# Spreading one small row over the partitions: a repeating DMA in place of a product with ones, a copy and a fill

## The chip, the cores and the metric

The kernel runs on one core of one Trainium2 chip. The profile names the core's parts: PE (matrix products; PEld is its weight load), DVE, ACT and POOL (elementwise engines), SP (it only issues transfers here), and 16 DMA engines that move data between HBM and the on-chip memories. ACT, POOL and SP each issue transfers from a queue of their own; the profile calls these ACTq, POOLq and SPq. The metric is the device time of one execution in microseconds, as the median of the runs. Before the change it is 176.96 us, the median of three runs that lie between 175.55 and 177.12.

## The reference

The inputs `r`, `k`, `v` have the shape (4, 8, 768, 48): batch, heads, time steps, head width. `w` and `u` have the shape (8, 48). Per batch and head a 48 x 48 state runs along time, and its result goes through a two-layer network with a piecewise gate:

```
for t in range(S):
    cur = einsum('bhd,bhe->bhde', u[None] * kt, vt)
    y[:, :, t] = einsum('bhd,bhde->bhe', rt, state + cur)
    state = w[None, :, :, None] * state + einsum('bhd,bhe->bhde', kt, vt)
x = y.transpose(0, 2, 1, 3).reshape(3072, 384)
h = x @ w_in                                   # 384 -> 2048
g = where(h >= 1, h, where(h <= -1, 0, (h + 1)**2 / 4))
out = g @ w_out                                # 2048 -> 384
```

`u` enters through the term of the current time step alone. It equals v times the sum over the head width of r * u * k, one number per time step and head.

## The kernel before

Time is cut into six chunks of 128 steps (`C`), and time lies on the 128 partitions. A group `g` is one chunk of two batches (`UNITS`), so there are 12 groups; a unit `n = 2 g + j` is one chunk of one batch. Inside a chunk the recurrence is written as matrix products: K is scaled by a table of falling powers of w (`Ks`), R by one of rising powers (`Rs`), both are transposed (`T`, copied out by `TT`), their product `A` is masked (`AT`) and multiplied with V (`Y`), and `Sp` with `Tm` and `decay` carries the state to the next chunk. The term with u is made without PE: `KU` = K * u, `RKU` = R * KU, `usum` sums over the head width, `V2` = V * that sum, and `y` adds it to `Y`. `X` and `xT` transpose y, `mm1` is the first layer (weights `w_in_sb`), `relu`, `square` and `gate` make the piecewise gate, `mm2` is the second layer (weights `w_out_sb`), `o` and `out` copy out and store.

The order of the work is written by hand. `ORDER` is a list of tokens `step.arguments@engine:buffer~fillers`, and the loop at the end of the kernel issues them one by one; each engine, and each queue of transfers, carries out its share of the list in that order. `~n` puts n matrix products of zeros ahead of a step. Each transfer from SP or ACT raises one of eight counters when it has landed, and the counters are handed out in turn; a transfer that uses a counter again waits until the earlier transfer on it has landed. The transfer of u has the counter DMAHW2, and the ninth load of SP's queue (`load.K.1.1`) is the next to use it.

u must stand on all 128 partitions, since time lies on them. The kernel loads the 384 values of u into one row (partition 96) of a tile of 97 rows, `u_row` (L151, L153, issued by ACT behind the transfer of w), and POOL fills the other 96 rows with zeros (L166). The step `bcu` (L242) multiplies it on PE by `ones`, a 97 x 128 tile that is one in row 96 and zero elsewhere, so that each of 128 result partitions holds u in float32. The step `u_bc` (L212, a call of `copy` on DVE) copies the result to the tile `u_bc`, which every `KU` reads (L337). The row of w goes a like way: ACT takes its logarithm into `lw_row` (`lw`, L232), `bcw` (L237) spreads it with the same `ones` into `wb`, and ACT makes the tables of powers from `wb` (`Wdn_p`, `Wup_p`, L257), which `Ks` and `Rs` (L327) of the first two groups multiply with.

The first lines of `ORDER` matter most here. SP loads V of groups 1 and 0, K and R of group 0, and so on, unit by unit for the first two groups (`NSPLIT`). DVE's share of the start is, in this order: fills, the copy to `u_bc`, `KU.0.0`, `Ks.0.0`, `RKU.0.0`, `Rs.0.0`, `Rs.0.1`, `KU.0.1`, `TT.0`. POOL's share is, after its fills: `KU.1.0`, three `RKU` with one `KU` between them, the mask `AT.0`, `Rs.2.0`, and then the transfers of `w_in`, whose issue stands in POOL's queue behind that product.

Of the kernel before, what the change touches and what calls it, by code (L numbers as in the profile page):

```python
# [8 lines left out]
F32 = mybir.dt.float32  # L9
# [5 lines left out]
P = 128  # L15
C = 128
HP = 64
ROWS = 97
# [14 lines left out]


ORDER = """
loadV.1.0:1 lw loadV.0.0:0 load.K.0.0:0 load.R.0.0:2 bcu:0 u_bc@D load.K.0.1 load.K.1.0:2 load.R.0.1 bcw:1 KU.0.0@D:0
Wdn_p:0 warm.6.h.1 wcol:0 V.0.0@A:4 V.1.0@A:2 Ks.0.0@D:2 load.R.1.0:0 Wup_p wCm load.K.1.1 RKU.0.0@D:1 Rs.0.0@D:1
Rs.0.1@D loadV.0.1 KU.0.1@D T.0:1 TT.0@D:0 Ks.0.1@D load.R.1.1 Ks.1.0@D:0 loadV.1.1 Wdn usum.0.0@D:1 A.0:2~2
Rs.1.0@D:0 KU.1.0@P:1 RKU.1.0@P:0 Ks.1.1@D AT.0.1:0 Sp.2:0~7 Rs.1.1@D KU.1.1@P load.R.2.0:1 Tm.2@D V.1.1@D T.2:1~4 Wup
# [64 lines left out]
def kernel(  # L104
# [11 lines left out]
    nc = tc.nc  # L116
    B, H, S, D = r.shape
    NP = H // 2
    DM = H * D
# [7 lines left out]
    const = ctx.enter_context(tc.tile_pool(name="const", bufs=1))  # L127
# [10 lines left out]
    def flat(x):  # L138
        return x.rearrange("p h d -> p (h d)")
# [4 lines left out]
    row = slice(ROWS - 1, ROWS)  # L144
    ones = const.tile([ROWS, P], F32, name="ones")
# [2 lines left out]
    lw_row = const.tile([ROWS, H, HP], F32, name="lw_row")  # L148
    nc.vector.memset(lw_row, 0.0)
    w_row = const.tile([ROWS, DM], F32, name="w_row")  # L150
    u_row = const.tile([ROWS, DM], F32, name="u_row")  # L151
    nc.scalar.dma_start(out=w_row[row], in_=w.rearrange("(o h) d -> o (h d)", o=1))
    nc.scalar.dma_start(out=u_row[row], in_=u.rearrange("(o h) d -> o (h d)", o=1))  # L153
    i_int = const.tile([P, 1], mybir.dt.int32, name="i_int")
    nc.gpsimd.iota(i_int, pattern=[[0, 1]], base=0, channel_multiplier=1)
    nc.scalar.preload_act_table_set("natural_log_exp_and_others")
# [6 lines left out]
        out=umask, in_=umask, compare_op=ALU.is_ge, fill=1.0,  # L163
        base=0, pattern=[[-1, P]], channel_multiplier=1,
    )
    nc.gpsimd.memset(u_row[: ROWS - 1], 0.0)  # L166
    i_col = const.tile([P, 1], F32, name="i_col")
    nc.vector.tensor_copy(i_col, i_int)
    up_col = const.tile([P, 1], F32, name="up_col")
# [15 lines left out]
    states_bf = [const.tile([P, NP, 2 * D], BF16, name="state_bf", tag=f"sb{b}") for b in range(B)]  # L185
    Wup = const.tile([P, H, D], F32, name="Wup")
    Wdn = const.tile([P, H, D], F32, name="Wdn")
    u_bc = const.tile([P, H, D], F32, name="u_bc")

    tiles = {}  # L190
    engines = {"D": nc.vector, "P": nc.gpsimd}

    def bank(i, shape, dtype, name):
        return psum(f"bank{i}", shape, dtype, name)
# [3 lines left out]
    def psum(tag, shape, dtype, name):  # L198
        t = ps.tile(shape, dtype, name=name, tag=tag)
        if idle[0]:  # L200
            flat = t if len(shape) == 2 else t.rearrange("p a b -> p (a b)") if len(shape) == 3 else t.rearrange("p a b c -> p (a b c)")
            flat = flat[:, : P if dtype == F32 else 2 * P]
            for _ in range(idle[0]):
                nc.tensor.matmul(flat if dtype == F32 else flat.bitcast(F32), zeros, zeros, start=True, stop=True)
            idle[0] = 0
        return t
# [4 lines left out]
    def copy(e, out, in_):  # L211
        nc.scalar.copy(out, in_) if e == "A" else engines[e].tensor_copy(out, in_)  # L212
# [24 lines left out]
        nc.tensor.matmul(tiles["wb"], ones, lw_row[:, :, :D], start=True, stop=True)  # L237

    @step
    def bcu(e, bk):  # L240
        tiles["ub"] = bank(bk[0], [P, DM], F32, "ub")
        nc.tensor.matmul(tiles["ub"], ones, u_row, start=True, stop=True)  # L242

    @step
    def wup(e, bk):
        nc.scalar.activation(flat(Wup), flat(tiles["wb"]), AF.Exp, scale=up_col, bias=0.0)

    @step
    def wdn(e, bk):
        nc.scalar.activation(flat(Wdn), flat(tiles["wb"]), AF.Exp, scale=dn_col, bias=0.0)  # L250

    do["Wup"], do["Wdn"] = wup, wdn


    def table(what, i, col):
        t = tiles["tab"][:, i, :DM].rearrange("p (h d) -> p h d", h=H)
        nc.scalar.activation(flat(t), flat(tiles["wb"]), AF.Exp, scale=col, bias=0.0)  # L257
        tiles["tab", what] = t
# [6 lines left out]
    @step  # L265
    def Wup_p(e, bk):
        table("R", 1, up_col)

    @step
    def u_bc_(e, bk):  # L270
        copy(e, flat(u_bc), tiles["ub"])

    @step
    def wcol(e, bk):
# [335 lines left out]
    for token in ORDER.split():  # L610
        token, _, idles = token.partition("~")
        idle[0] = int(idles or 0)
        name, _, bufs = token.partition(":")
        name, _, e = name.partition("@")
# [35 lines left out]
```

## Time and profile before

| what | value |
| --- | --- |
| median of three runs | 176.96 us (176.96, 175.55, 177.12) |
| the profiled execution's own time | 175.69 us |
| its span | 174.0 us |
| PE busy in the span | 163.9 us (94%) |
| DVE, ACT, POOL busy | 137.3, 135.5, 107.8 us (79%, 78%, 62%) |
| share of the DMA engines: SP's queue, POOL's queue, ACT's queue | 73.3%, 11.5%, 0.2% |
| moved by DMA | 28.78 MB, mean 165 GB/s |
| granted clock of PE | 1.0 in all 40 slices |

All times within the execution are counted from the start of the span. A row of the timeline gives start, duration, engine, line, operation, output and inputs, and in brackets the idle time of the engine before it with what ended that idle time. A row of the chain of waits gives start, duration and the engine and line on which the end then depends; that chain is followed back from the last instruction. In a table of windows the columns are the window and its length, the busy time and number of instructions of PE, PEld, DVE, ACT and POOL, the granted clock, the busy share of the DMA engines (over 1.0 where packets overlap) and the rate in GB/s.

### The profile page before, as it was taken

To read this page: it belongs to the slowest core of one execution; us is meant where nothing else is said; L and a number is where in the kernel's file an instruction comes from. 1 tells how busy PE (TensorE), PEld (TensorE's weight loads), DVE (VectorE), ACT (ScalarE), POOL (GpSimd) and SP (SyncE) were. 2 spreads that over 40 slices of the span, in tenths; PEclk is the share of its full clock that TensorE was granted. 3 is DMA by queue.
4 is the path that set the end of the run, shared out by engine and by line. 5 is a ranking of instruction groups with operands and counts; after the bars stand their busy time and mean duration, and the time that the engine had idled before them with its cause. 6 is when DMAs were issued, how large, how long until landed. Compare 5 with 4: busy or idle time off the path is not lost.

```text
span 174.0 us, 4223 instructions
## 1 busy us (share of the span) xinstructions
PE 163.9 (94%) x1713; PEld 126.0 (72%) x1713; DVE 137.3 (79%) x177; ACT 135.5 (78%) x187; POOL 107.8 (62%) x88
## 2 busy tenths in 40 slices
PE   2969889999899999999999999999999999999993
PEld 1758779976677767687877976867778677778672
DVE  5689789986998977978989969897788998555530
ACT  4567979898769979359897997896797868899921
POOL 6087998804997994999967998777939200000000
PEclk9999999999999999999999999999999999999999
DMA  5999999999989999899998999989864910400222
GB/s 109 219 200 229 197 195 190 193 197 179 205 177 196 263 225 226 158 230 180 152 189 154 179 231 238 203 186 234 166 120 98 262 24 4 136 0 4 90 90 90
DMA packets 107367, 28.78 MB, mean 165 GB/s; under 512 B 100946, under 2 KB 106964, under 8 KB 107348
## 3 DMA queue, kind: packets, MB, share of 16 engines
q1 hardware_dynamic: 103888, 25.24, 73.3%
q0 software_dynamic: 3312, 3.15, 11.5%
q8 instruction: 13, 0.21, 0.5%
q10 hardware_dynamic: 148, 0.13, 0.2%
q14 instruction: 6, 0.05, 0.1%
HBM read 20.45 MB, written 4.72 MB: 145 GB/s over the span
## 4 chain that ended last, share of the span: by engine, by line
PE 75%; DVE 7%; DMA 6%; ACT 5%; SPq 3%; issue 2%; POOL 1%; ACTq 0%; POOLq 0%
PE op L554 33%; PE hp L526 31%; PE A L406 4%; DMA w_in_sb<-in_moe_w_in_dram 3%; ACT sq L539 3%; SPq L304 3%; DMA R<-in_r_dram 2%; PE Y L446 2%; DVE gt L544 2%; PE Y L441 2%; DVE AT L421 2%; PE Sp L432 2%; ACT pt L534 2%; POOL Rs L327 1%; PE T L388 1%
## 5 line engine op out<-in xcount | busy, mean ns | idle before, releaser
L544 DVE SCALAR_TENSOR_TENSOR gt<-sq,hp 128x1024 bf16<-128x1024 f32 x48 | 58.2, 1216 | 18.1 <-ACT sq L539 17.2
L526 PE MATMUL hp<-xT,w_in_sb 128*128 128x256 bf16 (+1 forms) x600 | 69.1, 268 | 1.1 <-DMA w_in_sb<-in_moe_w_in_dram 0.8
L554 PE MATMUL op<-w_out_sb,gt 128*128 128x384 bf16 (+2 forms) x400 | 68.9, 320 | 0.1
L526 PEld LDWEIGHTS <-w_in_sb 128*128 128x128 bf16 x600 | 55.7, 98 | 9.5 <-DMA w_in_sb<-in_moe_w_in_dram 1.0
L534 ACT ACTIVATE pt<-hp 128x1024 f32<-128x1024 f32 x48 | 48.7, 1021 | 9.0 <-PE hp L526 8.7
L539 ACT ACTIVATE sq<-pt 128x1024 f32<-128x1024 f32 x48 | 50.7, 1058 | 4.9 <-DVE gt L544 3.9
L554 PEld LDWEIGHTS <-gt 128*128 128x128 bf16 x400 | 37.2, 98 | 20.4
L421 DVE TENSOR_TENSOR AT<-A,umask 128x1024 bf16<-128x1024 f32 x22 | 26.3, 1217 | 1.8 <-PE A L406 1.7
L327 POOL TENSOR_TENSOR Rs<-Wup,R 128x768 bf16<-128x768 f32 x10 | 19.0, 1896 | 8.4 <-DMA R<-in_r_dram 7.4
L344 POOL TENSOR_TENSOR RKU<-R,KU 128x768 f32<-128x768 f32 (+1 forms) x11 | 17.9, 1635 | 1.8 <-DVE KU L337 0.9
L369 POOL TENSOR_TENSOR V<-V,diag 128x768 f32<-128x768 bf16 (+1 forms) x10 | 14.1, 1410 | 7.9 <-ACT V L212 7.4
L489 POOL TENSOR_TENSOR state<-Tm,wCm 128x384 f32<-128x384 f32 x16 | 16.6, 1048 | 3.1 <-DVE Tm L476 3.0
L337 POOL TENSOR_TENSOR KU<-K,u_bc 128x768 f32<-128x768 f32 (+1 forms) x9 | 14.9, 1654 | 4.8 <-DMA K<-in_k_dram 4.7
L327 POOL TENSOR_TENSOR Ks<-Wdn,K 128x768 bf16<-128x768 f32 x9 | 16.4, 1826 | 1.0 <-DMA K<-in_k_dram 1.0
L212 ACT COPY oo<-op 128x384 f32<-128x384 f32 x19 | 9.0, 474 | 9.1 <-PE op L554 8.3
L468 DVE TENSOR_TENSOR yy<-Y,V 128x384 bf16<-128x384 f32 x18 | 9.7, 551 | 2.3 <-issue 1.9
L357 DVE TENSOR_REDUCE diag<-RKU 128x16 f32<-128x768 f32 (+1 forms) x13 | 11.0, 851 | 0.0
L446 PE MATMUL Y<-V,AT 128*128 128x48 bf16 x192 | 10.8, 183 | 0.1
L212 ACT CAST V<-VF 128x768 bf16<-128x768 f32 (+1 forms) x12 | 8.9, 747 | 1.2 <-PE Y L446 1.2
L476 DVE TENSOR_TENSOR Tm<-Sp,state 128x384 f32<-128x384 f32 x16 | 8.7, 550 | 1.4 <-PE Sp L432 1.4
L446 PEld LDWEIGHTS <-AT 128*128 128x128 bf16 x192 | 9.4, 96 | 0.6 <-POOL AT L416 0.2
L441 PE MATMUL Y<-state_bf,RT 128*128 128x96 bf16 x72 | 8.3, 204 | 0.0
(85 smaller groups left out, 140.8 us busy)
## 6 DMA issues: line engine op xcount, KB each, us to landing
out_dram<-oo SPq DMA_DIRECT2D x11, 384.0 KB, 3.1
R<-in_r_dram SPq DMA_DIRECT2D x10, 384.0 KB, 4.7
K<-in_k_dram SPq DMA_DIRECT2D x10, 384.0 KB, 5.3
VF<-in_v_dram SPq DMA_DIRECT2D x10, 384.0 KB, 4.4
w_out_sb<-in_moe_w_out_dram POOLq DMA_DIRECT2D x4, 384.0 KB, 8.8
VF<-in_v_dram SPq DMA_DIRECT2D x4, 192.0 KB, 3.4
K<-in_k_dram SPq DMA_DIRECT2D x4, 192.0 KB, 3.8
R<-in_r_dram SPq DMA_DIRECT2D x4, 192.0 KB, 3.7
```

The costliest lines, as they stand in the source:

```text
L212: nc.scalar.copy(out, in_) if e == "A" else engines[e].tensor_copy(out, in_)
L327: engines[e].tensor_mul(of_unit(dst, j0, j1)[:, :, :, :D], rep(tab, j1 - j0), of_unit(tiles[what, g], j0, j1))
L337: engines[e].tensor_mul(of_unit(tiles["KU", g], j0, j1), of_unit(tiles["K", g], j0, j1), rep(u_bc, j1 - j0))
L344: engines[e].tensor_mul(of_unit(tiles["RKU", g], j0, j1), of_unit(tiles["R", g], j0, j1), of_unit(tiles["KU", g], j0, j1))
L421: nc.vector.tensor_mul(t.rearrange("p i n t -> p (i n) t"), tiles.pop(("A", n)).rearrange("p i n t -> p (i n) t"), umask.unsqueeze(1).to_b ...
L446: nc.tensor.matmul(t[:, 2 * p + i, :], tiles["AT", n][:, i, p, :], tiles["V", g][:, j * H + 2 * p + i, :], start=(c == 0), stop=True, skip ...
L489: nc.gpsimd.tensor_mul(states[(g % BP) * UNITS + j], tiles.pop(("Tm", n)), wCm)
L526: nc.tensor.matmul(hp[:, f, cols], w_in_sb[:, i, n0 : n0 + P], tiles["xT", g][:, units, i, :], start=(i == 0), stop=(i == nK - 1), skip_gr ...
L534: nc.scalar.activation(tiles["pt", g, q], tiles["hp", g, q], AF.Relu, bias=0.5, scale=0.5)
L539: nc.scalar.activation(tiles["sq", g, q], tiles.pop(("pt", g, q)), AF.Square, bias=0.0)
L544: nc.vector.scalar_tensor_tensor(out=gt, in0=tiles.pop(("sq", g, q)), scalar=1.0, in1=tiles.pop(("hp", g, q)), op0=ALU.min, op1=ALU.max)
L554: nc.tensor.matmul(t, tiles["gt", g, q][:, f, j * P : (j + 1) * P], w_out_sb[:, n, cols], start=(n == 0), stop=(n == nF - 1),)
```

## The change

The transfer of `u` into one row is replaced by a transfer that reads the row of 384 values 128 times, once for each partition, straight into `u_bc`; ACT issues it at the same place, behind the transfer of w. The tile `u_row`, its fill on POOL, the step `bcu` on PE and the step `u_bc` on DVE are gone, and so are their two tokens in `ORDER`. Nothing else in `ORDER` differs.

```diff
 ORDER = """
-loadV.1.0:1 lw loadV.0.0:0 load.K.0.0:0 load.R.0.0:2 bcu:0 u_bc@D load.K.0.1 load.K.1.0:2 load.R.0.1 bcw:1 KU.0.0@D:0
+loadV.1.0:1 lw loadV.0.0:0 load.K.0.0:0 load.R.0.0:2 load.K.0.1 load.K.1.0:2 load.R.0.1 bcw:1 KU.0.0@D:0
...
     w_row = const.tile([ROWS, DM], F32, name="w_row")
-    u_row = const.tile([ROWS, DM], F32, name="u_row")
     nc.scalar.dma_start(out=w_row[row], in_=w.rearrange("(o h) d -> o (h d)", o=1))
-    nc.scalar.dma_start(out=u_row[row], in_=u.rearrange("(o h) d -> o (h d)", o=1))
+    u_bc = const.tile([P, H, D], F32, name="u_bc")
+    nc.scalar.dma_start(out=u_bc.rearrange("p h d -> p (h d)"), in_=u.rearrange("(o h) d -> o (h d)", o=1).to_broadcast([P, DM]))
...
-    nc.gpsimd.memset(u_row[: ROWS - 1], 0.0)
...
-    u_bc = const.tile([P, H, D], F32, name="u_bc")
...
     @step
-    def bcu(e, bk):
-        tiles["ub"] = bank(bk[0], [P, DM], F32, "ub")
-        nc.tensor.matmul(tiles["ub"], ones, u_row, start=True, stop=True)
...
-    @step
-    def u_bc_(e, bk):
-        copy(e, flat(u_bc), tiles["ub"])
```

PE's first instructions before the change; L242 is `bcu`, L237 is `bcw`, L608 are the fillers `warm.6`, and the brackets name what an instruction waits for:

```order
L645 UNCONDITIONAL_BRANCH [waits barrier_Pool_Activation_PE_DVE_SP_release]
L242 MATMUL ub<-u_row,ones 128x384 [waits DMAHW2_49,DVE_49,Pool_49]
L237 MATMUL wb<-lw_row,ones 128x384 [waits Activation_49]
L608 LDWEIGHTS zeros
L608 MATMUL idle<-zeros 128x128
```

And after it, where the line numbers of the changed file are lower by up to 11:

```order
L634 UNCONDITIONAL_BRANCH [waits barrier_Pool_Activation_PE_DVE_SP_release]
L235 MATMUL wb<-lw_row,ones 128x384 [waits Activation_49]
L597 LDWEIGHTS zeros
L597 MATMUL idle<-zeros 128x128
L597 LDWEIGHTS zeros
```

`bcw` is now PE's first product, and PE no longer waits for the transfer of u.

DVE's instructions from the last fill to the first copy of transposes, before the change; DMAHW4 is the counter of `load.K.0.0`, DMAHW0 at that place that of `load.R.0.1`:

```order
L179 MEMSET wCm 128x384
L212 COPY u_bc<-ub 128x384 [waits PE_49]
L337 TENSOR_TENSOR KU<-K,u_bc 128x384 [waits DMAHW4_49,DVE_49]
L327 TENSOR_TENSOR Ks<-tab,K 128x8x48 [waits Activation_49]
L344 TENSOR_TENSOR RKU<-R,KU 128x384 [waits DMAHW5_49,DVE_49]
L327 TENSOR_TENSOR Rs<-tab,R 128x8x48 [waits Activation_49]
L327 TENSOR_TENSOR Rs<-tab,R 128x8x48 [waits DMAHW0_49]
L337 TENSOR_TENSOR KU<-K,u_bc 128x384 [waits DMAHW6_49]
```

And after it:

```order
L178 MEMSET wCm 128x384
L326 TENSOR_TENSOR KU<-K,u_bc 128x384 [waits DMAHW4_49,DMAHW2_49]
L316 TENSOR_TENSOR Ks<-tab,K 128x8x48 [waits Activation_49]
L333 TENSOR_TENSOR RKU<-R,KU 128x384 [waits DMAHW5_49,DVE_49]
L316 TENSOR_TENSOR Rs<-tab,R 128x8x48 [waits Activation_49]
L316 TENSOR_TENSOR Rs<-tab,R 128x8x48 [waits DMAHW0_49]
L326 TENSOR_TENSOR KU<-K,u_bc 128x384 [waits DMAHW6_49]
L210 COPY TT<-T 128x1024 [waits PE_49]
```

The copy to `u_bc` is gone from DVE, and the first `KU` (`KU.0.0`) now waits for the transfer of u itself (DMAHW2) beside that of K.

More of the change, by code (lines that the diff above doesn't have):

```diff
@@ L267, in Wup_p @@
         table("R", 1, up_col)
-    @step
-    def u_bc_(e, bk):
-        copy(e, flat(u_bc), tiles["ub"])
     @step
```

## The prediction

> **What bounds the kernel now.** I read first the page's summary of the chain that ended last, then that chain in order of time up to 46 us, then the windows of the start, then the timeline of the start. The summary, shares of the span by engine:
>
> ```profile
> PE 75%; DVE 7%; DMA 6%; ACT 5%; SPq 3%; issue 2%; POOL 1%; ACTq 0%; POOLq 0%
> ```
>
> Three quarters of the chain are PE, but the edit touches only the first 6 us, so what counts is where the chain runs early. The same chain in order of time, start and duration:
>
> ```profile
> 4.63 0.81 SPq L304
> ...
> 5.49 3.73 DMA R<-in_r_dram
> ...
> 9.24 0.56 DVE Rs L327
> 9.80 0.47 DVE KU L337
> 10.27 0.61 DVE TT L212
> ...
> 10.93 0.61 PE A L406 x6
> ...
> 16.43 1.77 POOL Rs L327
> 18.20 5.91 DMA w_in_sb<-in_moe_w_in_dram
> ...
> 24.16 0.84 PE hp L526 x12
> ```
>
> Up to 5.49 the chain is SP's issuing of loads. Then it is the landing of `load.R.0.1` at 9.22 (5.49 + 3.73), DVE's `Rs.0.1`, `KU.0.1` and `TT.0`, the product `A.0`, and later the landing of `w_in` at 24.11 (18.20 + 5.91), on which the first `mm1` waits. From there to 45 us it alternates between ACT and DVE, then PE carries it to the end. The start is thus bound by transfers. The windows confirm it (the last three columns are the clock, the share of the DMA engines and GB/s):
>
> ```profile
> 0.00:2.00 2.00, 0.00 (x0) 0.00 (x0) 0.88 (x5) 0.36 (x1) 1.16 (x9) 1.00 0.01 3
> 2.00:4.00 2.00, 0.77 (x1) 0.50 (x2) 1.47 (x11) 1.45 (x2) 1.85 (x6) 1.00 1.02 202
> 4.00:6.00 2.00, 2.00 (x5) 0.89 (x4) 0.73 (x2) 0.00 (x0) 0.00 (x0) 1.00 1.10 215
> ...
> 8.00:10.00 2.00, 1.59 (x12) 1.11 (x12) 1.31 (x3) 1.58 (x5) 0.99 (x1) 1.00 1.08 214
> ```
>
> The DMA engines start about 2 us into the span and have no gap from there on. Loads of 192 KB (196,608 bytes) go through at 214 GB/s (the last row), 0.92 us each. Any bytes put in front of `load.R.0.1` delay it.
>
> **The change, part by part.** The timeline of the start holds all that is removed and what waits for it:
>
> ```profile
> 0.81 0.54 ACTq L152 DMA_DIRECT2D w_row<-in_w_dram  x1
> 1.39 0.23 ACTq L153 DMA_DIRECT2D u_row<-in_u_dram  x1
> 1.64 1.28 ACT L156 ACT_TABLE_LOAD   x1 [1.64 <-PEq L634]
> 2.00 0.42 POOL L166 MEMSET u_row<- 96x384 f32 x1
> 2.94 0.52 ACT L232 ACTIVATE lw_row<-w_row 1x384 f32<-1x384 f32 x1
> 3.23 1.62 PE L242 MATMUL ub<-u_row,ones 97*128 97x384 f32 x2 [3.23 <-DMA u_row<-in_u_dram]
> 4.64 1.48 PE L237 MATMUL wb<-lw_row,ones 97*128 97x384 f32 x2
> 4.88 0.56 DVE L212 COPY u_bc<-ub 128x384 f32<-128x384 f32 x1 [1.34 <-PE ub L242]
> 5.83 0.56 DVE L337 TENSOR_TENSOR KU<-K,u_bc 128x384 f32<-128x384 f32 x1 [0.39 <-DMA K<-in_k_dram]
> 6.17 0.56 ACT L257 ACTIVATE tab<-wb,dn_col 128x384 f32<-128x384 f32 x1 [2.71 <-PE wb L237]
> 6.75 0.56 DVE L327 TENSOR_TENSOR Ks<-tab,K 128x384 bf16<-128x384 f32 x1 [0.37 <-ACT tab L257]
> 7.47 0.77 SPq L304 DMA_DIRECT2D K<-in_k_dram  x1
> 8.16 0.56 DVE L327 TENSOR_TENSOR Rs<-tab,R 128x384 bf16<-128x384 f32 x1 [0.38 <-ACT tab L257]
> 8.56 0.99 POOL L337 TENSOR_TENSOR KU<-K,u_bc 128x384 f32<-128x384 f32 x1 [4.71 <-DMA K<-in_k_dram]
> 9.24 0.56 DVE L327 TENSOR_TENSOR Rs<-tab,R 128x384 bf16<-128x384 f32 x1 [0.53 <-DMA R<-in_r_dram]
> ```
>
> *POOL's fill, 0.42 us:* worth nothing. POOL's next product waits 4.71 us for K anyhow.
>
> *DVE's copy, 0.56 us:* worth nothing. It ends at 5.44, and `KU.0.0` waits 0.39 us more, for K.
>
> *PE's `bcu`, 1.62 us:* it goes, and `bcw` can start when `lw` is done (2.94 + 0.52 = 3.46) and not at 4.64. The tables follow about 1.1 us sooner. On DVE this takes away two waits for tables, of 0.37 and 0.38 us. Neither reaches the chain: `Rs.0.1` still waits for its own load, and had 0.53 us of idle time before it already; `TT.0`, which `A.0` needs, stands behind it on DVE. Worth nothing here. What is late next is `load.R.0.1`, which was late before.
>
> *The new transfer's issue on ACT:* the nearest row is ACT's store of 128 x 1024 bytes at the end.
>
> ```profile
> L600 ACTq DMA_DIRECT2D out_dram<-o_sb x1: 377/377/377, 170.7 to 170.7; - x1
> ```
>
> It is 0.38 us where 0.23 us stood, so the table load, `lw` and `bcw` move 0.15 us later. At the upper end is the 0.77 us of SP's issue of as many bytes in shorter packets at 7.47, which is 0.54 us later. Either lies within the 1.1 us that `bcu` gives back; without that cover it would still meet the 0.53 us of idle time before `Rs.0.1`.
>
> *The new transfer's bytes:* 128 x 1536 = 196,608 bytes in place of 1,536. The lower end is nothing (the engines' overlap takes it up; no gain, since no byte less is moved). The upper end is the 0.92 us of a load of the same size. Nearest in packet size are the stores of the output at the end, alone on the DMA engines, whose rows are also 1,536 bytes:
>
> ```profile
> 168.00:169.00 1.00, 1.00 (x12) 0.82 (x11) 0.06 (x1) 0.00 (x0) 0.00 (x0) 1.00 0.98 359
> ```
>
> At 359 GB/s, 196,608 bytes are 0.55 us of all 16 engines. I take this. On the path it is whole: the transfer is issued at 1.39, when three of the loads ahead of `load.R.0.1` have not been issued, and the engines were already full. The Trainium skill ("DMA: Bandwidth & Descriptors", Where 436 GB/s comes from) puts the ceiling of the fabric at 435 GB/s; by it the term would be 0.45 us, an estimate. The row is measured on this kernel's own packets, so it stands.
>
> *The new wait:* `KU.0.0` waits for `u_bc` as well. Behind it on DVE stand `Ks.0.0`, `RKU.0.0`, `Rs.0.0` and `Rs.0.1`, and PE's transposes wait for these. SP's `load.K.1.1` (7.47) waits for the same counter, with the rest of the loads behind it. The landing of such transfers, and of the larger one that follows:
>
> ```profile
> K<-in_k_dram SPq DMA_DIRECT2D x4, 192.0 KB, 3.8
> ...
> R<-in_r_dram SPq DMA_DIRECT2D x1, 384.0 KB, 4.8
> ```
>
> So u lands at about 1.39 + 3.8 = 5.2, at worst 6.2. K itself, 0.55 us later, now lands at about 6.4. `KU.0.0` to `Rs.0.0` are four products of 0.56 us, 2.2 us, and must be done by 9.24 + 0.55 = 9.8; they may start as late as 7.5. No cost.
>
> *Whether 0.55 us survives to the end:* `load.R.2.0` is issued at 11.47 and takes 4.8 us, landing at about 16.3; `Rs.2.0` on POOL starts at 16.43, `w_in` is issued behind it at 18.20 and lands at 24.11. All of this is the same queue of bytes, with no gap in it, and moves along. After 24.16 the chain that I read is a string of steps, each released by the one before it; no step in it is released by something that the new transfer leaves where it was. Nothing that I see absorbs the term.
>
> The sum: 174.0 + 0.55 = 174.55 of span, and 175.69 + 0.55 = 176.24 for an execution like the profiled one. That one lies 1.27 under the median of 176.96. The four times known (175.55, 175.69, 176.96, 177.12) fall into two pairs, so the median of three lands near either. I add the term to their mean: 176.33 + 0.55 = 176.9.
>
> **The rivals.** *Hidden (chance 0.18).* The 16 engines take the new packets in between, and `load.R.0.1` lands when it did: 176.3. For it speaks that shares over 1.0 show overlapping packets, against it that the rate stays at 202 to 215 GB/s as if at its limit.
>
> *The row is read one packet at a time (0.06), the slow side.* All 128 reads go to the same 1,536 bytes. In the window of the stores a packet takes 16 x 0.98 us / (359,000 / 1,536) = 67 ns of an engine; if the reads cannot overlap, 128 x 67 ns = 8.6 us. They begin about 1.15 us after the issue, as SP's first load does (issued at 0.81, the DMA engines busy from 2), so u lands at 1.39 + 1.15 + 8.6 = 11.1 us. From a landing at 7.5 on, every microsecond costs one: `Rs.0.1` would start at 11.1 + 2.2 = 13.3 and not 9.24, which is 4.1 us, 180.4 in all. Against it: w's row, one packet, has landed when `lw` starts at 2.94. No row shows one address read many times.
>
> *PE comes to full speed later (0.11) or earlier (0.09).* PE waits 1.33 us before `A.0`, works on without a gap, and at about 14.6 us its rate nearly doubles:
>
> ```profile
> 10.93 0.61 PE L406 MATMUL A<-TT 48*128 48x128 bf16 x8 [1.33 <-DVE TT L212]
> ...
> 14.21 0.62 PE L388 MATMUL T<-ident,Rs 128*128 128x128 bf16 x4
> ...
> 14.84 0.39 PE L204 MATMUL Sp<-zeros 128*128 128x128 bf16 x4
> ```
>
> ```profile
> 11.00:14.60 3.60, 3.60 (x39) 3.40 (x40) 3.60 (x9) 2.47 (x4) 3.60 (x5) 1.00 1.09 219
> 14.60:18.20 3.60, 3.35 (x66) 2.85 (x64) 3.49 (x7) 3.00 (x10) 2.62 (x3) 1.00 1.23 229
> ```
>
> The same 3.6 us hold 39 products, then 66, though the granted clock reads 1.00 in both. With 1.62 us of PE work gone from the start, the doubling could come a stretch later or, by chance, earlier. One such stretch is worth at most 3.6 x (1 - 39/66) = 1.5 us: 176.9 + 1.5 = 178.4, or 175.4. Against a full price: part of PE's work there waits for `w_in` anyway. The Trainium skill ("TensorE: Matmul & The Clock Gate", What's actually happening) says that the clock is released after a busy window of about 3.4 us that runs freely, not from the kernel's start. The trace agrees on the length (10.93 to 14.6 is 3.7 us); by that rule the step depends on the run's phase more than on the edit, and one window would be 1.4 us, an estimate.
>
> **How the numbers follow.** The forecast has the rest, 0.56. A measurement of this kernel can tell about 1% (1.8 us) from no change. Its own runs differ by almost that. Faster by over 1%: half of the earlier speed, and 0.04 for a hidden transfer with a median in the lower pair, 0.09. Slower by over 1%: the late row 0.06, two thirds of the later speed 0.07, and 0.02 for a median in the upper pair with the full 0.92 us, 0.15. Within 1%: 0.76. The range: at the top 178.4, and 0.3 for most of the upper end of the transfer, 178.7; at the bottom between 175.4 and the 174.9 that follows when the transfer is also free, 175.2. Outside lie the late row and the ends of both clock cases.
>
> **What would show it.** In the profile after: `u_bc` on ACT's queue with an issue of about 0.4 us; `bcw` at about 3.6 and the first table at about 5.1; `KU.0.0` at about 6.4, released by K; `Rs.0.1` at about 9.8, still released by its load; `w_in` landing at about 24.7; the span 174.5. I am wrong if `KU.0.0` is released by `u_bc` later than 7.5, if `Rs.0.1` starts at 9.24 or before, or if the first `mm1` is not later although `Rs.0.1` is.

## The result, and the profile after

The changed kernel is slower: 1.0068 times the time before, 95% interval 1.0040 to 1.0096. The median is 177.37 us against 175.73 us, with 20 runs of each; on 175.73 us the ratio is 1.2 us, 0.7 to 1.7. The profiled executions, each one run only, are 176.87 and 175.69 us, with spans of 175.1 and 174.0. The measured median lies within the predicted range of 175.2 to 178.7, but the forecast of 176.9 us lay a hair below the median then known (176.96), so that as a number it forecast no slowing. The ratios compare fast runs alone: four of the changed kernel's 20 (178.54, 178.62, 179.15 and 423.85 us) were slow, and so was the profiled execution of one experiment (b1), of which only the start is read below.

The page after, its span, the chain by engine and ACT's queue (q10: packets, MB, share), where before stood 148 packets, 0.13 MB, 0.2%:

```profile
span 175.1 us, 4217 instructions
...
q10 hardware_dynamic: 290, 0.33, 0.6%
...
PE 72%; DMA 6%; SPq 6%; DVE 6%; ACT 5%; issue 2%; POOL 1%; POOLq 0%; ACTq 0%
```

SP's issuing (SPq) has doubled its share of the chain, from 3% to 6%. The timeline of the start after the change shows why:

```profile
1.38 0.38 ACTq L153 DMA_DIRECT2D u_bc<-in_u_dram  x1
2.79 2.21 SPq L293 DMA_DIRECT2D R<-in_r_dram  x1
3.66 1.65 PE L235 MATMUL wb<-lw_row,ones 97*128 97x384 f32 x2 [3.66 <-ACT lw_row L230]
5.05 1.55 SPq L293 DMA_DIRECT2D K<-in_k_dram  x2
5.34 0.56 ACT L250 ACTIVATE tab<-wb,dn_col 128x384 f32<-128x384 f32 x1 [1.74 <-PE wb L235]
6.64 1.85 SPq L293 DMA_DIRECT2D R<-in_r_dram  x2
6.83 0.56 DVE L326 TENSOR_TENSOR KU<-K,u_bc 128x384 f32<-128x384 f32 x1 [3.30 <-DMA K<-in_k_dram]
10.37 0.56 DVE L316 TENSOR_TENSOR Rs<-tab,R 128x384 bf16<-128x384 f32 x1 [1.33 <-DMA R<-in_r_dram]
```

And the row of before that answers to the second of these:

```profile
2.80 0.71 SPq L304 DMA_DIRECT2D R<-in_r_dram  x1
```

The issue of `load.R.0.0` takes 2.21 us in place of 0.71, and every load after it is issued later: `load.R.0.1` at 6.64 and not at 5.49. `Rs.0.1` starts at 10.37 and not at 9.24, 1.13 us later, still released by its load. All else at the start came nearly as worked out: the issue on ACT takes 0.38 us, `bcw` starts at 3.66, the table is made at 5.34 (5.1 was forecast), and `KU.0.0` at 6.83 (6.4) is released by K and not by u.

The windows of the start after the change; the last columns are clock, share of the DMA engines and GB/s:

```profile
2.00:4.00 2.00, 0.34 (x1) 0.34 (x2) 1.46 (x11) 1.59 (x2) 1.49 (x5) 1.00 0.90 208
4.00:6.00 2.00, 2.00 (x10) 1.21 (x9) 0.00 (x0) 0.63 (x2) 0.00 (x0) 1.00 0.94 190
6.00:8.00 2.00, 1.63 (x10) 1.55 (x10) 1.17 (x3) 0.95 (x3) 0.00 (x0) 1.00 1.00 199
```

The engines had more to move, and were less busy: 0.90 and 0.94 of their time in the first two windows against 1.02 and 1.10 before. In the first they moved about as much as before (208 and 202 GB/s), in the second less (190 and 215). Further on the chain after the change reads:

```profile
12.19 4.59 DMA R<-in_r_dram
...
16.94 1.75 POOL Rs L316
18.70 6.72 DMA w_in_sb<-in_moe_w_in_dram
...
25.46 0.84 PE hp L515 x12
```

The chain takes another way than before: up to 12.14 us it is SP's issuing, one load after the other, then the landing of `load.R.2.0` (issued at 12.19 and not at 11.47), for which `Rs.2.0` now waits; `Rs.0.1` and `A.0` are no longer on it. `Rs.2.0` has made up part of the delay (0.51 us late), but the first `mm1` is 1.30 us late: `w_in` lands 6.72 us after its issue in place of 5.91. It shares the engines with loads of SP that are themselves later, such as `load.K.2.0` (issued at 14.38 and not at 13.26); that this is why it takes longer is not shown. The span ends 1.1 us later.

### The profile page after: what moved, and what is told of

It is laid out like the page before. It is cut to its first block, busy times and chain, and to the rows that moved or that the text cites. A ratio compares the mean times of both kernels' runs of the same rounds, so it can differ in the third digit from the quotient of the medians.

```text
span 175.1 us, 4217 instructions
## 1 busy us (share of the span) xinstructions
PE 163.4 (93%) x1711; PEld 126.2 (72%) x1711; DVE 136.4 (78%) x176; ACT 135.4 (77%) x187; POOL 107.3 (61%) x87
## 4 chain that ended last, share of the span: by engine, by line
PE 72%; DMA 6%; SPq 6%; DVE 6%; ACT 5%; issue 2%; POOL 1%; POOLq 0%; ACTq 0%
PE op L543 33%; PE hp L515 31%; SPq L293 6%; DMA w_in_sb<-in_moe_w_in_dram 4%; PE A L395 3%; ACT sq L528 3%; DMA R<-in_r_dram 3%; DVE gt L533 2%; PE Y L435 2%; PE Y L430 2%; DVE AT L410 2%; ACT pt L523 2%; PE Sp L421 1%; POOL Rs L316 1%; DVE V L210 1%
```

## The experiments

In all of them Rs.0.1's start is read, 9.24 before and 10.37 after the change, as the place where the start's delay is seen; three kernels without the repeating transfer at the start (a2, b4, c3) show it at 9.43, 9.28 and 9.11, so differences under about 0.3 us say nothing.

**a1: the removed work put back.**

```diff
-load.R.0.0:2 load.K.0.1
+load.R.0.0:2 bcu:0 u_bc@D load.K.0.1
...
+    u_row = const.tile([ROWS, DM], F32, name="u_row")
+    u_spare = const.tile([P, H, D], F32, name="u_spare")
+    nc.gpsimd.memset(u_row, 0.0)
...
+        nc.tensor.matmul(tiles["ub"], ones, u_row, start=True, stop=True)
...
+        copy(e, flat(u_spare), tiles["ub"])
```

> The changed kernel with the removed work put back on spare tiles: POOL fills a row tile with zeros, bcu multiplies it, DVE copies the result to a tile that nobody reads. u still comes by the repeating transfer. Theory that the removed work was hidden and that the transfer alone makes the change: Rs.0.1 starts at 10.4 us as after the change, span 175.1, 0.7% over before. Rival, that the removal of bcu takes PE's early work away and so delays its full speed: the full speed comes back at about 14.6 us and the span falls towards 174.0.

Ratio 1.0094 (1.0060 to 1.0128), span 175.7. With `bcu`, the copy and the fill back in their places, the loss stays. The removed work does not carry it. Rs.0.1 is later than expected, and the last two rows belong to PE:

```profile
2.80 2.20 SPq L305 DMA_DIRECT2D R<-in_r_dram  x1
...
10.96 0.56 DVE L328 TENSOR_TENSOR Rs<-tab,R 128x384 bf16<-128x384 f32 x1 [2.05 <-DMA R<-in_r_dram]
...
15.07 0.63 PE L389 MATMUL T<-ident,Rs 128*128 128x128 bf16 x4
...
15.89 0.39 PE L389 MATMUL T<-ident,Rs 128*128 128x128 bf16 x4
```

The held issue is there again, 2.20 us. That Rs.0.1 starts 0.59 us later than after the change, with the same transfer, is not explained: like transfers can differ by that much at this place, or the work put back costs it. PE comes to full speed at about 15.9 us, some 2.3 us sooner than after the change (below), and the time is no shorter, so the rival falls.

**a2: without the repeating transfer.**

```diff
-    nc.scalar.dma_start(out=u_bc.rearrange("p h d -> p (h d)"), in_=u.rearrange("(o h) d -> o (h d)", o=1).to_broadcast([P, DM]))
+    nc.scalar.dma_start(out=u_row[row], in_=u.rearrange("(o h) d -> o (h d)", o=1))
...
+    nc.gpsimd.memset(u_bc, 0.1)
```

> The changed kernel without the repeating transfer: ACT loads u into one row as before the change (nobody reads it) and POOL fills u_bc with a constant, so the term with u is computed with 0.1 in place of u. bcu and the copy stay away. Theory that the transfer alone makes the change: SP's issue of load.R.0.0 takes 0.7 us again, Rs.0.1 starts at 9.2, span 174.0, ratio to before 1.000. Rival, that the missing PE work makes it: span stays at about 175.1, ratio about 1.007, though Rs.0.1 starts at 9.2.

Ratio 0.9996 (0.9965 to 1.0027), span 174.4. The loss is gone, and no gain is in its place: the 1.62 us of `bcu` and the copy were hidden to within 0.3%, as the prediction had it. (POOL fills a tile here too, so the fill is not tested.) The transfer alone makes the change. Its rows:

```profile
2.90 0.71 SPq L295 DMA_DIRECT2D R<-in_r_dram  x1
...
9.43 0.56 DVE L318 TENSOR_TENSOR Rs<-tab,R 128x384 bf16<-128x384 f32 x1 [1.34 <-DMA R<-in_r_dram]
```

The load is issued in 0.71 us, and DVE waits 1.34 us for `load.R.0.1`: the tables that come sooner only lengthen this wait.

**a3: the transfer on SP's queue; a4: on POOL's.** My theory after the result was that the two queues of ACT and SP get into each other's way. In a3 SP issues the transfer, between `loadV.0.0` and `load.K.0.0`; in a4 POOL does, where its fill of the row stood.

```diff
-loadV.0.0:0 load.K.0.0:0
+loadV.0.0:0 uload load.K.0.0:0
...
-    nc.scalar.dma_start(out=u_bc.rearrange("p h d -> p (h d)"), in_=u.rearrange("(o h) d -> o (h d)", o=1).to_broadcast([P, DM]))
+        nc.sync.dma_start(out=flat(u_bc), in_=u.rearrange("(o h) d -> o (h d)", o=1).to_broadcast([P, DM]))
```

```diff
-    nc.scalar.dma_start(out=u_bc.rearrange("p h d -> p (h d)"), in_=u.rearrange("(o h) d -> o (h d)", o=1).to_broadcast([P, DM]))
...
+    nc.gpsimd.dma_start(out=u_bc.rearrange("p h d -> p (h d)"), in_=u.rearrange("(o h) d -> o (h d)", o=1).to_broadcast([P, DM]))
```

> The same repeating transfer of u, but issued by SP between its second and third load, so that it stands in the queue of the loads and not in ACT's. Theory that a second queue with long packets holds up SP's issue (load.R.0.0 took 2.21 us to issue in place of 0.71): no issue on SP takes over 1.3 us, Rs.0.1 starts at 9.24 + 0.55 = 9.8 and the span is 174.5. Rival, that the bytes or the one address cost 1.1 us in whatever queue: Rs.0.1 at 10.4, span 175.1.

> The same repeating transfer of u, issued by POOL where its fill of the row stood (at 2.0 us). Theory that the hold-up comes from two queues whose descriptors the same hardware makes (ACT and SP): SP's issues stay under 1.3 us, Rs.0.1 starts at about 9.8, span 174.5, unless u itself lands later than 7.5. Rival, that any second queue with long packets starves the loads, or that the one address does: an SP issue of over 2 us or Rs.0.1 at 10.4, span 175.1.

Both start Rs.0.1 later than ACT's queue does, at 11.58 (a3) and 11.60 us (a4) against 10.37. The ratios are 1.0138 (1.0095 to 1.0180) and 1.0114 (1.0065 to 1.0163); they too are higher, but their intervals overlap that of the change. The theory of two queues falls: in a3 the transfer stands in the queue of the loads itself, and the hold-up is larger. The timeline and the windows of a3:

```profile
1.94 0.76 SPq L246 DMA_DIRECT2D u_bc<-in_u_dram  x1
...
3.85 4.01 SPq L296 DMA_DIRECT2D K<-in_k_dram  x2
...
11.58 0.56 DVE L319 TENSOR_TENSOR Rs<-tab,R 128x384 bf16<-128x384 f32 x1 [1.29 <-DMA R<-in_r_dram]
```

```profile
4.00:6.00 2.00, 2.00 (x12) 1.46 (x10) 0.00 (x0) 1.04 (x3) 0.00 (x0) 1.00 0.53 94
```

and the same window of a4:

```profile
4.00:6.00 2.00, 2.00 (x12) 1.47 (x10) 0.00 (x0) 1.05 (x3) 0.24 (x1) 1.00 0.71 129
```

For two microseconds the engines work half of their time, or 71% of it, while loads wait behind. So it is neither the bytes (engines would be full) nor the queue. By the packet records of the traces the 128 packets of u go from 2.88 to 4.60 us on ACT's queue (the changed kernel), and from 3.51 to 6.88 us on SP's (a3). What is left is the long packets, or that all 128 read one place.

**b1 and b2: the same transfer, from 128 different rows.** Bytes, packets, queue and place are the same; the source is the first 128 rows of the second layer's weights, which are also 384 float32 long. b1 makes this edit in the changed kernel, b2 in a3.

```diff
-in_=u.rearrange("(o h) d -> o (h d)", o=1).to_broadcast([P, DM])
+in_=moe_w_out[:P, :]
```

> The changed kernel, where the same transfer on ACT's queue (128 packets of 1,536 bytes) reads 128 different rows of the second layer's weights and not 128 times the row of u; the term with u is then computed with these rows in u's place. Theory that the one address is what holds the engines up: they do not starve, SP's issue of load.R.0.0 takes under 1.3 us and not 2.21, Rs.0.1 starts at 9.24 + 0.55 = 9.8 at most, span 174.5, ratio to before about 1.003. Rival, that long packets in front of or between the short ones do it: SP's issue takes 2.2 us again, Rs.0.1 at 10.4, span 175.1, ratio 1.007 to 1.009.

> The kernel that issues the transfer from SP between its second and third load, with 128 different rows of the second layer's weights in place of the one row of u (the term with u is computed with them). With the row of u, Rs.0.1 started at 11.58, the engines were busy 53% of the window from 4 to 6 us, and the span was 176.8. Theory of the one address: Rs.0.1 at 9.8 at most, the window over 95% busy, span 174.5. Rival, long packets in whatever queue: Rs.0.1 at 11.6 and about 53% as with u.

b1: ratio 1.0007 (0.9970 to 1.0043); b2: 1.0049 (1.0009 to 1.0088), where a3 had 1.0138. The start of b1:

```profile
2.74 1.41 SPq L293 DMA_DIRECT2D R<-in_r_dram  x1
...
9.68 0.56 DVE L316 TENSOR_TENSOR Rs<-tab,R 128x384 bf16<-128x384 f32 x1 [1.26 <-DMA R<-in_r_dram]
```

and the window of b2 that answers to a3's, with its Rs.0.1:

```profile
4.00:6.00 2.00, 2.00 (x12) 1.46 (x10) 0.00 (x0) 1.04 (x3) 0.00 (x0) 1.00 1.08 252
```

```profile
9.90 0.56 DVE L319 TENSOR_TENSOR Rs<-tab,R 128x384 bf16<-128x384 f32 x1 [1.20 <-DMA R<-in_r_dram]
```

Only the source differs, and the window goes from 94 to 252 GB/s; a3's time and b2's lie apart by more than their intervals. So the cause is shown: all 128 packets read the one row of u. Whether any other row read 128 times would do the same, or the place of u in memory has a part in it, no run tried. SP's issue in b1 is still 1.41 us, a little over the 1.3 that I set; that much I put down to the bytes. Of the 1.13 us by which Rs.0.1 is late after the change, 9.68 - 9.24 = 0.44 us are bytes and 10.37 - 9.68 = 0.69 us the one address. This split rests on one execution of each: with a1's Rs.0.1 the second part would be 10.96 - 9.68 = 1.28 us, and on SP's queue the parts are 0.66 and 1.68 us (a3, b2).

**b3: half of the reads.**

```diff
-    nc.scalar.dma_start(out=u_bc.rearrange("p h d -> p (h d)"), in_=u.rearrange("(o h) d -> o (h d)", o=1).to_broadcast([P, DM]))
+    nc.scalar.dma_start(out=u_bc[:HP].rearrange("p h d -> p (h d)"), in_=u.rearrange("(o h) d -> o (h d)", o=1).to_broadcast([HP, DM]))
...
+    nc.gpsimd.memset(u_bc[HP:], 0.1)
```

> The changed kernel with u read 64 times and not 128, for partitions 0 to 63; POOL fills the other 64 partitions with 0.1 in place of u. Theory of the one address, served at a rate of its own: half of the delay of Rs.0.1 goes, 10.37 to about 9.8, span 174.5. Rival, a cost per transfer that does not depend on its reads: Rs.0.1 stays at 10.4.

Ratio 1.0033 (1.0002 to 1.0065), Rs.0.1 at 9.62. More than half of the delay goes (0.38 us are left of 1.13), so it is no fixed cost per transfer; the time alone would not show it, since its interval overlaps that of the change. Whether the delay falls in proportion can't be read from it, with 0.3 us between like executions.

**c3: the transfers alone.** Into the kernel before, late, where the DMA engines are empty, behind `square.10.1`, `square.10.2`, `relu.11.0` and `relu.11.1` on ACT:

```diff
+    def probe(e, bk, i):
+        n = (P, P, HP, 16)[i]
+        nc.scalar.dma_start(out=probes[i][:n], in_=moe_w_out[:n, :] if i == 1 else row_of_u)
```

> The kernel before the change, with four more transfers of 1,536-byte packets issued by ACT late, where the DMA engines are empty (151 to 162 us): the row of u 128 times, then 128 different rows of the second layer's weights, then the row of u 64 times, then 16 times, each into a tile that nobody reads. It measures the disputed cost by itself. Theory of the one address: the 128 different rows move at 359 GB/s or more, in about 0.55 us, like the stores; the row of u at 114 GB/s or less, as in the changed kernel (128 packets in 1.7 us), so 1.7 us or more; 64 times in half of that, 16 times within 0.3 us. Rival, that one address only matters beside other reads: all of them move at the same rate, and the two transfers of 128 packets take the same time to land.

Two windows of c3, within the transfer of the row of u and within that of the different rows:

```profile
152.20:153.60 1.40, 1.40 (x14) 1.12 (x12) 1.21 (x1) 1.37 (x2) 0.00 (x0) 1.00 0.37 124
154.40:155.00 0.60, 0.60 (x5) 0.35 (x4) 0.60 (x1) 0.60 (x1) 0.00 (x0) 1.00 0.64 236
```

With nothing beside it the one row moves at 124 GB/s, the engines idle for 63% of the time. That is 1,536 / 124 = 12.4 ns for a packet. By the packet records the four transfers take 1.72, 1.01, 0.90 and 0.24 us: half the reads take about half the time. So the one address slows a transfer by itself, not only beside other reads; the rival falls. The different rows missed what I expected of them: 1.01 us and not 0.55; why, no run shows. The changed kernel's transfer of u also took 1.72 us, 13 ns a packet, but that agreement is in part luck: there 87 of the 128 reads began within the first 0.6 us, here 53 of them, and the other 41 straggled. So 12 to 13 ns is a mean and not a fixed pace of the one address.

**b4: the first transfer of w_in ahead of Rs.2.0,** in the kernel before, to see whether the order of bytes at the start holds a gain.

```diff
-AT.0.0 Rs.2.0@P:1 A.2:1 w_in.0 TT.1@A:2
+AT.0.0 w_in.0 Rs.2.0@P:1 A.2:1 TT.1@A:2
```

> The kernel before the change, with the first transfer of w_in issued by POOL ahead of Rs.2.0 and not behind it. It tests whether the start is a queue of bytes up to the landing of w_in. If so, w_in.0 is issued at about 15.5 and not at 18.2, the first mm1 starts up to 2.4 us earlier (xT.0 is ready at 21.7), the loads of group 2 land later, and the span falls by 1 to 2 us, to 172 to 173. Rival, that what comes after the first mm1 is bound by ACT and DVE or by the loads put behind: the first mm1 is earlier, but the span stays at 174.0 within 0.5.

Ratio 0.9997 (0.9963 to 1.0032), span 174.2: no gain. `w_in.0` is issued at 15.50, and the first `mm1` starts at 23.31 and not at 24.16, but the chain now runs through ACT:

```profile
23.78 0.45 ACT RKU L355 x4
24.23 0.37 ACT xT L212
...
25.27 0.56 DVE y L468
```

`y.3` starts at 25.27, where before the change it started at 25.46. So the chain through ACT's sums and copies is only some 0.2 us shorter than the one through the landing of `w_in`, and binds when that is gone. No kernel tried is clearly faster than the one before the change.

## Why the prediction was right or wrong

- **What bounds the start: right.** It is the queue of bytes up to `load.R.0.1` and on to `w_in`. Every kernel that delayed the loads by much was slower. At its end another chain stands close: b4 finds ACT's only 0.2 us shorter.
- **The removed work is worth nothing: right.** a2 shows it for `bcu` and the copy, 0.9996; a1 shows that putting all of it back changes nothing that can be measured.
- **Issue on ACT, the new wait, the landing of u: right.** 0.38 us as priced; u landed 3.5 us after its issue, at 4.9; `KU.0.0` was released by K.
- **The bytes, 0.55 us: the step that failed.** "I take this" rested on stores of the same packet size. The bytes alone cost 0.44 us at `Rs.0.1` (b1), so the row was fit for that. But the upper end, 0.92 us, was the price of a load from different addresses, and the transfer cost 1.13 us there in the profiled execution. The step took the engines to stay full while they read the one row; they did not (0.90 and 0.94 busy after the change, 0.53 in a3). The missing term is the one address, 0.69 us by b1, more by a1. The price of the whole, 1.2 us (0.7 to 1.7), is about twice what was forecast.
- **The rival "the row is read one packet at a time" (0.06): near the mechanism, wrong in its size and its path.** It took the 67 ns that a packet occupies an engine as the pace. The mean is 12 to 13 ns: the reads of one row do not wait for each other's whole packet, but they stay below what the engines can do. At 1.7 us for 128 packets u lands before `KU.0.0` needs it, so the cost did not come by that rival's path (a late u) but through the loads that it slowed. I weighed the two ends, all bytes at full rate or one packet at a time, and no case between.
- **"Moves along" to the end: right in sign.** 1.13 us at `Rs.0.1`, 0.51 at `Rs.2.0`, 1.30 at the first `mm1`, 1.1 in the span. It is luck that the first and the last are alike: half of the delay was absorbed on the way, and `w_in`'s longer landing, 6.72 in place of 5.91 us, for which the prediction has no term, brought 0.8 us. That 0.44 us at `Rs.0.1` in b1 ends as 0.07% (up to 0.43%) can't be told from 0.25%.
- **PE's full speed comes later: it did in the profiled execution, and it cost nothing to be seen.** Two equal groups of products of the changed kernel:

```profile
17.36 0.61 PE L395 MATMUL A<-TT 48*128 48x128 bf16 x8
...
18.59 0.40 PE L395 MATMUL A<-TT 48*128 48x128 bf16 x8
```

  The rate changes at about 18.2 us and not at 14.6. But in c3, whose start is that of the kernel before, PE ran at full speed at 7.75, then at half again until about 13.9 (the single row below them is a window, with the granted clock at 0.50):

```profile
7.75 0.38 PE L388 MATMUL T<-ident,Ks 128*128 128x128 bf16 x4
...
12.38 0.63 PE L204 MATMUL T<-zeros 128*128 128x128 bf16 x4
...
13.96 0.39 PE L388 MATMUL T<-ident,Rs 128*128 128x128 bf16 x4
```

```profile
11.00:13.00 2.00, 2.00 (x25) 1.80 (x22) 2.00 (x6) 1.56 (x3) 2.00 (x3) 0.50 1.10 213
```

  Its span is 174.1, that of before 174.0. The same instructions got their speed at other times, as the rule on the free-running window in the Trainium skill ("TensorE: Matmul & The Clock Gate", What's actually happening) has it, and the end did not move. Nor does the loss follow the speed: a1 had it back at 15.9 and lost as much. The price of 1.5 us was a bound for work on the path; the start's path is made of transfers.
- **The time itself: a second step that failed.** The term was added to the mean of four executions (176.33) and not to the median it was to be compared with. That put a slowing of 0.55 us a hair below the time before. With 20 runs the median before is 175.73; the four lay a little high. And 0.7% could be told from no change, where the prediction set about 1%.

Left open: why the 128 packets took 3.4 us in SP's queue, where the loads stand behind them in the same queue, against 1.7 us in ACT's; why in ACT's the first two thirds of the reads were fast; and which part of the memory holds up the one row. No run tells these apart.

## What to carry to other kernels

Do not price a transfer that repeats its source by its bytes: measure it in an empty stretch, as c3 does, and beside the transfers it will meet, as b1 and b2 do. In this kernel, whose start waits for loads, a step on an idle engine that saves bytes was free, and a repeating transfer in its place was not, from any of three queues. And add a term to the same figure that the result will be held against.

## What the runs showed of the hardware

- Reads of one row of 1,536 bytes, 128 times: 124 GB/s alone, the engines 37% busy, against 236 GB/s in a like window for 128 different rows (c3). Beside other loads it takes them along: 94 GB/s in all in a window of 2 us against 252 GB/s (a3, b2).
- The issue of two loads by SP lasted 4.01 us (a3) where 1.90 us stood before, and 2.17 us where only the source of the transfer ahead of them was another (b2). A long issue was here a sign of slow transfers ahead, not of much to issue.
- The doubling of PE's rate came at about 14.6, 13.9 and 18.2 us (before, c3, after). In c3, where PE had already run at full speed, the column of the granted clock shows the half rate, 0.50 from 11 to 13 us; before and after the change it reads 1.00 all through the first stretch at half rate, and only the durations of equal products show it.
